# Attention scores in four 64-column matmuls a group instead of eight of 32 columns

## The chip, the core and the metric

The kernel runs on one core of one Trainium2 chip. The metric is the device time of one execution in microseconds; the kernel before takes 1029.15 us (the median of 3 runs, 1028.61 to 1029.83). The core has TensorE (PE in the profile; its weight loads are shown apart, as PEld), VectorE (DVE), ScalarE (ACT), GpSimd (POOL) and SyncE (SP, which here issues DMAs).

## What is computed

For 2048 tokens x of width 512, a gate g mixes an attention block with 32 query heads, one shared key head and one shared value head of 16 columns each, and a feed-forward block:

```
g = sigmoid(sum(x * gate_w))                       # one number per token
q = x @ wq  (32 heads x 16)   k = x @ wk (16)   v = x @ wv (16)
p = softmax(q k^T / 4)                              # per head 2048 x 2048
a = (p v, heads side by side) @ wo
b = silu(x @ w1) @ w2                               # 512 -> 1792 -> 512
out = g * a + (1 - g) * b
```

All of it is float32, and the kernel keeps nearly that accuracy by splitting operands into two 16-bit parts.

## The kernel before, in words

The attention is done in 16 rounds: 4 chunks of 512 tokens times 4 blocks of 8 heads. One round goes through the 2048 keys in 32 steps of 64 keys, and each step does four of the eight heads at a time, twice: `p` counts these half steps, 2 x 32 x 16 = 1024 in all. For each p:

- `scores(p)` (line 1186) writes a PSUM tile `S` of 128 x 1024 float32: the scores of 64 keys for four heads and 512 tokens. The keys `KT` are the weights (the stationary operand), the queries `qb` stream through. One head needs a contraction over 50 rows (16 numbers of q in split parts, and shift rows), so two heads stand in the array one above the other, at rows 0 to 63 and 64 to 127 (index `f`). In the kernel before, a matmul has 50 rows and 32 columns of weights and occupies a tile of 64 rows by 32 columns of the array; eight of them (four column places `m`, two row places `f`) fill the array. Places m = 0 and 1 hold the two halves of the 64 keys for one pair of heads, m = 2 and 3 the same keys for the other pair: they differ only in which part of `qb` they stream. There are two `S` tiles, so scores(p) waits until the exponential of p - 2 has read its own.
- `exponential(p)` (line 1192, on ACT) writes exp of it to a buffer `P` of SBUF.
- `low` (line 1198, on DVE) makes the low part of some of these for a product in two 16-bit parts, and `pv` (line 1223) multiplies by the values, either in float32 or in such parts: weights `VF` or `VP`, 64 rows by 32 columns, again eight tiles filling the array. For a whole step that is 8 matmuls (or 16, in two row halves).

The feed-forward products, the query projections and the output projections run in between. They too are cut into 64 x 32 tiles: `product` (line 832) issues, for four column places, a matmul of a new output on the upper 64 rows and one of an older output on the lower 64 rows. So in the main part of the kernel all matmuls of TensorE, of whatever kind, use tiles of 64 rows by 32 columns, and one pass of eight matmuls streams 512 columns through the full array. `product` and `pv` aren't touched by the change.

Only near the start are there other tile shapes between groups of scores: `begin()` makes the values (128 x 32 tiles, line 1247), transposes them (128 x 64, line 1258) and places the keys (64 x 128, lines 352 and 353), and `early_products()` makes three projections with the whole array (128 x 128, line 836).

What runs when is set at build time. A planner in `attention()` keeps a clock for PE, ACT and DVE, adds assumed durations for each piece (`PASS_S` for a group of scores, `PASS` for a pass, `EXP` for an exponential), and writes the instructions of each engine in the resulting order; on the chip, semaphores alone hold the engines together. The planner's constants are the same in both kernels, and so is the order of everything other than the matmuls and weight loads of the scores.

The last 12 groups of scores (the branch `s >= ends_at`, line 1179) are laid out by token halves and are left as they were. So 1012 of the 1024 groups are concerned. A second pass for inputs out of range stands behind a branch and is not run on these inputs.

Of the kernel before, what the change touches and what calls it, by code (L numbers as in the profile page):

```python
# [53 lines left out]
def kernel(  # L54
# [21 lines left out]
    nc = tc.nc  # L76
# [15 lines left out]
    KT = consts.tile([128, S], F16)  # L92
# [30 lines left out]
    sc = consts.tile([128, 96], F32)  # L123
# [667 lines left out]
    def attention(ctx, scale_of, t_scale, shifts, split_pieces, chores, q_todo, early, gates_):  # L791
# [363 lines left out]
        pvs, state, Os, qtile = {}, {}, {}, {}  # L1155
# [12 lines left out]
        def scores(p):  # L1168
            s, j = divmod(p, 2)
            i, kt = steps[s]  # L1170
            sc = banks[p] = pS.tile([128, 2, 512], F32, name="S")
            if s >= ends_at:
                u, q = (s - ends_at) % PAIRS, (s - ends_at) // PAIRS
                for a in range(2):
                    for m in range(4):
                        for f in range(2):
                            b = 64 * f
                            k0 = (NK - 2 * PAIRS + 2 * u + a) * 64 + 32 * (m % 2)
                            nc.tensor.matmul(sc[32 * m:32 * m + 32, f, 256 * a:256 * a + 256], KT[b:b + 50, k0:k0 + 32],  # L1179
                                             qtile[i][b:b + 50, m // 2, j, 256 * q:256 * q + 256], start=True, stop=True)  # L1180
                return
            for m in range(4):
                for f in range(2):
                    b = 64 * f
                    k0 = kt * 64 + 32 * (m % 2)
                    nc.tensor.matmul(sc[32 * m:32 * m + 32, f], KT[b:b + 50, k0:k0 + 32], qtile[i][b:b + 50, m // 2, j], start=True, stop=True)  # L1186

        def exponential(p):
            s, j = divmod(p, 2)
# [365 lines left out]
        def on_pe(t, x):  # L1555
            _, _, kind, s = x
            length = PASS
            if kind == "S":
                p = n_mm[0]
                i, k = steps[p // 2]  # L1560
                if k >= NKT and i + 1 < len(rounds) and i + 1 not in qtile and (not early or rounds[i + 1][::-1] in shifted):
                    prefetch(i + 1)
                if p % 2 == 0 and k == 0 and q_todo:
                    queue.append(q_todo.pop(0))
                scores(p)
                mm_done[p] = t + PASS_S + LATE
                n_mm[0] += 1
            elif kind == "R":
                length = next(begin_)
                n_begin[0] -= 1  # L1570
            elif kind == "E":
                next(whole_)
                n_early[0] -= 1
            elif kind == "F":
                work.go(t)
            else:
                length = do_pv(*s, t)
            work.others += kind in "SP"
            return length
# [120 lines left out]
```

## Time and profile before

| What | Value |
|---|---|
| median of 3 runs | 1029.15 us |
| profiled execution, first to last instruction | 1033.2 us |
| PE busy | 1012.3 us (98%) |
| ACT busy | 993.1 us (96%) |
| DVE busy | 916.4 us (89%) |
| POOL busy | 62.7 us (6%) |
| matmuls in the profile | 32605, of which 8096 are those of the changed line |
| granted clock of TensorE, mean | 0.998 of full speed |

The profiled execution took 4 us more than the median. In rows of groups, "64*32 64x512" means weights of 64 rows and 32 columns, and 512 streamed columns; busy time is the union of the instructions' spans, so for matmuls that run beside each other it is less than count times mean. The end of a matmul is modelled, while its start is recorded; where spacing matters, starts are read. "issue" as the end of an idle time means that the profile shows nothing that was waited for.

### The profile page before, as it was taken

The numbers are of one execution on the slowest core, as the hardware profiler recorded it, in microseconds if no ns is written. First come the engines' busy times: TensorE is split into PE (matmuls) and PEld (weight loads), VectorE is DVE, ScalarE is ACT, GpSimd is POOL, SyncE is SP. The second block draws the span as 40 slices with busy tenths as digits, with TensorE's granted clock in tenths as the row PEclk, the third lists the DMA queues.
The fourth block names the chain that finished last, engine by engine and source line by source line (L and its number), as shares of the span: only waits on it lengthen the run. The fifth ranks groups of instructions, "written<-read, shape, count | busy, mean of one in ns | idle before, by whom it ended". The sixth has DMA issues, their size and how long they took to land.

```text
span 1033.2 us, 69440 instructions
## 1 busy us (share of the span) xinstructions
PE 1012.3 (98%) x32605; PEld 615.0 (60%) x32605; DVE 916.4 (89%) x1191; ACT 993.1 (96%) x1109; POOL 62.7 (6%) x141
## 2 busy tenths in 40 slices
PE   8999999999999999999999999999999999999996
PEld 7345655565656666656566665566665565565563
DVE  7778887889899999999989899798999889989994
ACT  5899999999999999999999999999999999999994
POOL 5001111100000000000000000000000000000000
PEclk9999999999999999999999999999999999999999
DMA  5122322221011111100101110110111110100001
GB/s 207 53 76 65 93 58 61 70 62 19 15 19 41 39 36 30 20 20 15 35 16 35 50 30 20 30 25 10 34 32 25 33 48 10 35 10 14 10 4 47
DMA packets 28114, 40.12 MB, mean 39 GB/s; under 512 B 5689, under 2 KB 19370, under 8 KB 27818
## 3 DMA queue, kind: packets, MB, share of 16 engines
q0 software_dynamic: 10656, 15.73, 7.3%
q1 hardware_dynamic: 16442, 19.27, 5.9%
q8 instruction: 257, 4.21, 1.7%
q10 hardware_dynamic: 720, 0.59, 0.2%
q14 instruction: 39, 0.32, 0.1%
HBM read 19.98 MB, written 8.25 MB: 27 GB/s over the span
## 4 chain that ended last, share of the span: by engine, by line
PE 71%; issue 19%; ACT 6%; DVE 1%; DMA 1%; POOL 1%; SPq 0%; ACTq 0%; POOLq 0%; DVEq 0%
PE pm L832 26%; PE pv L1223 24%; PE S L1186 17%; ACT P L1192 4%; ACT xs L1192 1%; PE pm L836 1%; DMA xn<-in_A_x_dram 1%; PE pt L336 1%; POOL H L898 1%; PE pv L1211 1%; DMA H<-e 0%; ACT e L886 0%; DVE L L1198 0%; PE S L1179 0%; DVE e L889 0%
## 5 line engine op out<-in xcount | busy, mean ns | idle before, releaser
L1192 ACT ACTIVATE P<-S 128x1024 f32<-128x1024 f32 x764 | 731.4, 1081 | 11.8 <-PE S L1186 7.8
L1186 PE MATMUL S<-qb,KT 50*32 50x512 f16 x8096 | 471.6, 379 | 3.3 <-ACT P L1192 1.7
L1186 PEld LDWEIGHTS <-KT 50*32 50x32 f16 x8096 | 203.3, 90 | 186.6 <-issue 96.7
L1198 DVE TENSOR_TENSOR L<-P 128x1024 f16<-128x1024 f32 x242 | 288.8, 1216 | 20.0 <-ACT P L1192 16.7
L832 PE MATMUL pm<-xs,w1s 64*32 64x512 f16 x5376 | 274.9, 375 | 2.4 <-DVE e L889 1.7
L832 PE MATMUL pm<-w2s,H 64*32 64x512 f16 x5376 | 267.9, 375 | 2.0 <-DVE e L889 1.2
L1192 ACT ACTIVATE xs<-S 128x1024 f32<-128x1024 f32 x260 | 256.8, 1082 | 2.5 <-PE pv L1223 1.1
L1223 PE MATMUL pv<-P,VF 64*32 64x256 f32 (+1 forms) x4880 | 250.6, 450 | 0.3 <-issue 0.3
L832 PEld LDWEIGHTS <-w1s 64*32 64x32 f16 x5376 | 124.7, 92 | 49.8 <-issue 10.8
L832 PEld LDWEIGHTS <-H 64*32 64x32 f16 x5376 | 120.1, 93 | 44.3 <-issue 5.7
L1198 DVE TENSOR_TENSOR raw<-P 128x1024 f16<-128x1024 f32 x104 | 124.8, 1217 | 7.4 <-ACT P L1192 7.1
L1223 PEld LDWEIGHTS pv<-P,VF 64*32 64x32 f32 x4880 | 103.2, 106 | 32.6 <-issue 3.2
L1223 PEld LDWEIGHTS <-VP 64*32 64x32 f16 x3856 | 75.8, 92 | 34.3 <-issue 5.3
L1198 DVE TENSOR_TENSOR L<-xs 128x1024 f16<-128x1024 f32 x72 | 86.5, 1217 | 4.8 <-ACT xs L1192 4.5
L1223 PE MATMUL pv<-L,VP 64*32 64x512 f16 x1256 | 90.6, 375 | 0.0
L832 PE MATMUL pm<-xs,wqs 64*32 64x512 f16 x1152 | 87.0, 375 | 0.0
L1223 PE MATMUL pv<-P,VP 64*32 64x512 bf16 x1384 | 82.7, 387 | 0.0
L1198 DVE TENSOR_TENSOR raw<-xs 128x1024 f16<-128x1024 f32 x64 | 76.9, 1216 | 5.8 <-ACT xs L1192 5.5
L1223 PE MATMUL pv<-xs,VF 64*32 64x256 f32 (+1 forms) x1584 | 76.5, 416 | 0.1
L898 POOL DMA_DIRECT2D H<-e x56 | 30.1, 537 | 733.7 <-DVE e L889 723.2
L832 PE MATMUL pm<-wo_s,O 64*32 64x512 f16 x1440 | 70.4, 375 | 0.1
L1223 PE MATMUL pv<-raw,VP 64*32 64x512 f16 x672 | 54.8, 375 | 0.0
(216 smaller groups left out, 724.1 us busy)
## 6 DMA issues: line engine op xcount, KB each, us to landing
H<-e POOLq DMA_DIRECT2D x56, 128.0 KB, 2.5
raw<-in_B_w_dram POOLq DMA_DIRECT2D x24, 256.0 KB, 3.0
qb<-qd SPq DMA_DIRECT2D x180, 32.0 KB
xn<-in_A_x_dram SPq DMA_DIRECT2D x8, 512.0 KB
out_dram<-acc SPq DMA_DIRECT2D x14, 256.0 KB
qd<-qx SPq DMA_DIRECT2D x13, 256.0 KB
raw<-in_A_wo_dram POOLq DMA_DIRECT2D x4, 256.0 KB, 2.9
qb<-sh SPq DMA_DIRECT2D x60, 2.0 KB
```

Source lines behind the costliest of these rows:

```text
L336: nc.tensor.transpose(pt[:, kt], xn[c].rearrange("p t (d k) -> p t k d", k=KD)[:, t, kt], ident)
L832: nc.tensor.matmul(self.bank[32 * m:32 * m + 32], l(i, rows, 32 * m), r(j, rows), start=first, stop=last)
L836: nc.tensor.matmul(self.bank, l(i, slice(0, 128), 0, 128), r(j, slice(0, 128)), start=first, stop=last)
L898: nc.gpsimd.dma_start(H[:, 0], e)
L1186: nc.tensor.matmul(sc[32 * m:32 * m + 32, f], KT[b:b + 50, k0:k0 + 32], qtile[i][b:b + 50, m // 2, j], start=True, stop=True)
L1192: nc.scalar.activation(probs[s][:, 2 * j:2 * j + 2], banks.pop(p), AF.Exp, scale=scale_of(*rounds[steps[s][0]]))
L1198: nc.vector.tensor_tensor(lows[s, j], probs[s][:, js], upper(probs[s])[:, js], op=OP.subtract)
L1211: nc.tensor.matmul(pvs[i][h][32 * j:32 * j + 32, 256 * q:256 * q + 256], VF[r, NK - 2 * PAIRS + 2 * u + a], probs[s][r, j, 256 * a:256 * a ...
L1223: nc.tensor.matmul(pvs[i][h][32 * j:32 * j + 32, q], a[r], b[r, q], start=k == 0 and n != "B", stop=k == NK - 1 and n in "BMW")
```

## The change

Each of the 1012 groups is now four matmuls with 64 columns of weights each: place m = 0 holds all 64 keys of the step for the first pair of heads, m = 1 for the second pair. A matmul occupies a tile of 64 rows by 64 columns, and four of them fill the array. The scores come out in the same places of `S`, and what is streamed (512 columns for each matmul) is unchanged. A group has four matmuls and four weight loads in place of eight and eight; over the kernel 4048 matmuls and 4048 weight loads fall away.

```
-            for m in range(4):
+            for m in range(2):
                 for f in range(2):
                     b = 64 * f
-                    k0 = kt * 64 + 32 * (m % 2)
-                    nc.tensor.matmul(sc[32 * m:32 * m + 32, f], KT[b:b + 50, k0:k0 + 32], qtile[i][b:b + 50, m // 2, j], start=True, stop=True)
+                    nc.tensor.matmul(sc[64 * m:64 * m + 64, f], KT[b:b + 50, kt * 64:kt * 64 + 64], qtile[i][b:b + 50, m, j], start=True, stop=True)
```

No instruction changes its place: with the matmuls and weight loads of the scores left out, the order of every engine's instructions is the same before and after. In that order 998 groups of scores stand alone between other work of TensorE, and only seven times do two follow one another: 1005 stretches of scores. On 18 of them the work ahead, and on 20 the work behind, has one of the other shapes of the start; at all other borders it is a matmul of 64 x 32.

## The prediction

> **What bounds the kernel now.** I read the page's busy shares first, then the groups of instructions kept apart by form, then the timeline of PE and of its weight loads. The page:
>
> ```profile
> PE 1012.3 (98%) x32605; PEld 615.0 (60%) x32605; DVE 916.4 (89%) x1191; ACT 993.1 (96%) x1109; POOL 62.7 (6%) x141
> L1192 ACT ACTIVATE P<-S 128x1024 f32<-128x1024 f32 x764 | 731.4, 1081 | 11.8 <-PE S L1186 7.8
> ```
>
> Two engines look full. From the first group of scores to near the end (27.47 to 1012 us), in the view of busy time by stretch (us, then PE, PEld, DVE, ACT, POOL with their instructions, granted clock, DMA share, GB/s):
>
> ```profile
> 27.47:1012.00 984.53, 976.48 (x32008) 589.51 (x32007) 886.43 (x1111) 971.01 (x1076) 49.08 (x90) 1.00 0.14 34
> ```
>
> ACT is idle for only 984.5 - 971.0 = 13.5 us of it: ACT, with its 1024 exponentials, is what sets the pace. PE's busy time overstates its work, since the recorded span of a matmul overlaps the next. What PE needs is passes times spacing. The spacing, from starts in PE's timeline (start, us, what, count):
>
> ```profile
> 404.99 0.58 PE L1186 MATMUL S<-qb,KT 50*32 50x512 f16 x8
> 405.21 1.01 PE L832 MATMUL pm<-w2s,H 64*32 64x512 f16 x24
> 405.86 0.57 PE L1186 MATMUL S<-qb,KT 50*32 50x512 f16 x8
> 406.08 1.22 PE L832 MATMUL pm<-w2s,H 64*32 64x512 f16 x32
> 406.94 0.57 PE L1186 MATMUL S<-qb,KT 50*32 50x512 f16 x8
> ```
>
> Eight matmuls of 64 x 32 are one pass: a group of scores takes 405.21 - 404.99 = 0.22 us, three feed-forward passes 0.65 and four 0.86, so 0.216 each. A float32 pass over 512 columns takes twice that (from the next fence but one: 16 matmuls from 37.76 to 38.62, 0.43 each). The number of passes, by form (count | busy us, mean ns | idle before):
>
> ```profile
> L1186 PE MATMUL S<-qb,KT 50*32 50x512 f16 x8096 | 471.6, 379 | 3.3 <-ACT P L1192 1.7 <-ACT xs L1192 0.8 <-issue 0.3
> L832 PE MATMUL pm<-xs,w1s 64*32 64x512 f16 x5376 | 274.9, 375 | 2.4 <-DVE e L889 1.7 <-issue 0.4 <-DVE acc L813 0.2
> L832 PE MATMUL pm<-w2s,H 64*32 64x512 f16 x5376 | 267.9, 375 | 2.0 <-DVE e L889 1.2 <-issue 0.7
> L1223 PE MATMUL pv<-P,VF 64*32 64x256 f32 x3168 | 133.9, 375 | 0.3 <-issue 0.3
> L1223 PE MATMUL pv<-P,VF 64*32 64x512 f32 x1712 | 117.9, 589 | 0.0
> L1223 PE MATMUL pv<-L,VP 64*32 64x512 f16 x1256 | 90.6, 375 | 0.0
> L832 PE MATMUL pm<-xs,wqs 64*32 64x512 f16 x1152 | 87.0, 375 | 0.0
> L1223 PE MATMUL pv<-P,VP 64*32 64x512 bf16 x1384 | 82.7, 387 | 0.0
> L832 PE MATMUL pm<-wo_s,O 64*32 64x512 f16 x1440 | 70.4, 375 | 0.1
> L1223 PE MATMUL pv<-xs,VF 64*32 64x256 f32 x1280 | 55.8, 375 | 0.1
> L1223 PE MATMUL pv<-raw,VP 64*32 64x512 f16 x672 | 54.8, 375 | 0.0
> L1223 PE MATMUL pv<-xs,VP 64*32 64x512 bf16 x544 | 32.3, 387 | 0.0
> L1223 PE MATMUL pv<-xs,VF 64*32 64x512 f32 x304 | 20.9, 589 | 0.0
> ```
>
> Counts over 8: 1012 groups of scores x 0.22 = 222.6 us; line 832, 13344 matmuls, 1668 passes x 0.216 = 360.3; values over 256 float32 columns, 4448, 556 x 0.216 = 120.1; in 16-bit parts, 3856, 482 x 0.216 = 104.1; over 512 float32 columns, 2016, 252 x 0.43 = 108.4. Together 915.5 us; the small forms in the stretch (36 whole-array matmuls, values, keys, the tail's quarter groups) add under 20 by their counts. So of 984.5 us PE needs some 925 and has about **60 us of slack**, in small pieces: anything that costs PE less than 60 us in all can vanish behind ACT, and anything above shows.
>
> **The change, part by part.** Removed: 4048 matmuls and 4048 weight loads. The streamed columns stay 512 for each matmul, and four tiles of 64 x 64 fill the array as eight of 64 x 32 did, so a group remains one pass of 0.22 us; no columns of weights are saved either (4 x 64 = 8 x 32). ACT's and DVE's instructions are the same. So the part removed is worth at most ACT's 13.5 us of idle time; I take nothing, as ACT's waits for scores are 7.8 us in the row above.
>
> Added: the array's tile shape is now another in every group of scores than in the work around it. Before, all of the main part is 64 x 32, and the weights of the next pass are loaded while the current one streams. The trace has other shapes only near the start, and these are the rows that decide. First a change in the columns alone (64 x 32 to 64 x 128, as rows 64 stay), then to the whole array and back, then to 128 x 32 and back:
>
> ```profile
> 36.66 0.40 PE L1186 MATMUL S<-qb,KT 50*32 50x512 f16 x8
> 36.99 0.39 PE L352 MATMUL pm<-wo_s 64*128 64x512 f16 x1
> 37.22 0.38 PE L353 MATMUL pm<-wo_s 64*128 64x512 f16 x1
> 37.53 0.41 PE L1186 MATMUL S<-qb,KT 50*32 50x512 f16 x8
> 37.76 1.04 PE L1223 MATMUL pv<-P,VF 64*32 64x512 f32 x16
> 38.62 0.40 PE L1186 MATMUL S<-qb,KT 50*32 50x512 f16 x8
> ...
> 42.23 0.61 PE L836 MATMUL pm<-xs,wqs 128*128 128x512 f16 x2
> 42.76 0.41 PE L1186 MATMUL S<-qb,KT 50*32 50x512 f16 x8
> 43.10 0.82 PE L836 MATMUL pm<-xs,wqs 128*128 128x512 f16 x3
> 43.85 0.41 PE L1186 MATMUL S<-qb,KT 50*32 50x512 f16 x8
> 44.20 0.61 PE L836 MATMUL pm<-xs,wqs 128*128 128x512 f16 x2
> 44.73 1.09 PE L1223 MATMUL pv<-P,VF 64*32 64x512 f32 x16
> ```
>
> From 36.66 to 37.53 three passes stand: 3 x 0.216 = 0.648, but 0.87 went by: 0.222 us for two changes of shape, 0.111 each (the border S to L352 took 0.33 instead of 0.22, the border L353 to S 0.31). From 42.23 to 44.73 nine passes, 1.944 us of work in 2.50: 0.556 for five changes, 0.111 each. And
>
> ```profile
> 30.11 0.41 PE L1186 MATMUL S<-qb,KT 50*32 50x512 f16 x8
> 30.45 0.83 PE L1247 MATMUL pm<-xs,wo_s 128*32 128x512 f16 x12
> 31.22 0.41 PE L1186 MATMUL S<-qb,KT 50*32 50x512 f16 x8
> ```
>
> four passes in 1.11 us instead of 0.864: 0.246 for two, 0.123 each. None of these borders has a wait that the profile names. The weight loads show why (PEld, same times; second row a border without a change of shape):
>
> ```profile
> 36.99 0.09 PEld L352 LDWEIGHTS <-wo_s 64*128 64x128 f16 x1 [0.64 <-issue]
> 37.55 0.33 PEld L1223 LDWEIGHTS pv<-P,VF 64*32 64x32 f32 x16
> ```
>
> For L352 the load begins at 36.99, with its matmul, and only when the pass before has run out; the value weights begin at 37.55, 0.21 us ahead of their matmuls at 37.76. A change of shape lets no weights in ahead, and the array stands empty for a tenth of a microsecond.
>
> The Trainium skill states this as a rule that speaks against the change: "TensorEngine Tiling (Array Packing)", section Key Properties, says that changing the tiling mode, and not merely the tile, drains TensorE. The trace agrees for the three pairs of shapes above, at 0.11 to 0.12 us; no run here shows 64 x 64 beside 64 x 32 yet.
>
> The number of changes: 1005 stretches of scores have 2010 borders, 38 of which change the shape already; 1972 are new. 64 x 64 against 64 x 32 isn't in the trace. Its price lies between nothing (were it not another shape to the hardware) and the whole overlap of two passes (a matmul's 379 ns less the 216 of spacing, 0.163 us). I take 0.111, from the row that is nearest, 64 rows and other columns: **1972 x 0.111 = 219 us** of new work for PE.
>
> What hides it: PE's 60 us of slack. The gaps that PE makes for ACT (a score tile not yet read) close as ACT ceases to be the bound; gaps from other causes, like feed-forward results (2 us each in the rows of line 832) or the start, stay. I take 50 of 60 as used up. Then PE is the bound, ACT waits for scores, and the planned order, made for a pace that ACT sets, is merely late. DVE and the DMAs have no new work and gain time. Sum against the profiled execution: 1033.2 + 219 - 50 = 1202 us; the median stood 4 us below that execution, so **1198 us**. With 0.09 a change (just under the smaller border above) and all slack used, 1029 + 177 - 60 = 1146; with 0.123 and half of it, 1029 + 243 - 30 = 1242.
>
> **Rivals.**
>
> *No change of shape between 64 x 64 and 64 x 32* (ends on the other side). If the hardware keeps its weights-ahead when only the column count doubles within the same rows, nothing is added and 8096 fewer instructions go through PE; ACT loses some of its 13.5 us of idle time: 1018 to 1029, say 1027 us. It decides wherever a change costs below 60 / 1972 = 0.03 us. For it: the exact pair isn't in the trace. Against: the pair 64 x 32 and 64 x 128, rows alike, pays 0.111.
>
> *Only one direction pays*, as a 64 x 64 load may have to wait for two narrow tiles while a narrow load finds its tile free: 986 x 0.111 = 109, less 50: 1029 + 59 = 1088 us. Against: both borders paid in every row above (0.33 and 0.31 for 0.22).
>
> *The whole overlap is lost*, 0.163 a change, or the four wide loads, now exposed, are slower than the narrow ones: 321 - 50, 1300 us. Against: L352 and L353, with 128 columns of weights, start 0.23 apart and not later. "TensorE: Matmul & The Clock Gate", section Single matmul latency, of the Trainium skill gives a constant of about 166 ns beyond the streaming of a warm matmul; a full drain at each change would by that be an estimated 327 us. The trace's borders, 0.11, are below it.
>
> **How the numbers follow.** The main case has 0.80, no change of shape 0.08, one direction 0.06, the whole overlap 0.06. Predicted 1198 us; the main case's own bounds are 1146 to 1242, and the range, 1150 to 1250, holds most of that and leaves the three rivals out. 0.2% (2 us) is about what a measurement of this kernel can tell from no change. Faster by more comes from half of the second case, 0.04; within 0.2% from its other half, 0.04; slower 0.92.
>
> **What would show it.** PE matmuls fall to 32605 - 4048 = 28557. In the timeline a feed-forward pass to a group of scores takes 0.31, and scores to the next pass 0.33; weight loads of the scores begin with their matmuls, with idle time of PEld before them in nearly every group. ACT's busy time stays near 993 us but its share falls to about 83%, and its idle time, now some 200 us, is ended by PE's scores. If instead the borders read 0.22 with loads ahead, the first rival holds; if they read 0.33 but the span rose by far less than 170 us, the slack was mis-sized; borders of 0.38 mean the whole overlap.

## The result, and the profile after

The changed kernel takes 1248.75 us (median of 4 runs, 1248.57 to 1249.66) against 1028.88 us before, measured with it (median of 4 runs): 1.2142 times as long, 95% interval 1.2126 to 1.2159. The prediction was 1198 us with a range of 1150 to 1250, so the direction and the cause were right and the loss came out 220 us instead of 169. That the time still lies inside the range, 1 us below its upper end, is luck: it is above the 1242 us that the forecast gave as the upper bound of its main case.

From the page of the changed kernel (lines as before, less one from line 1186 on):

```profile
PE 1231.5 (99%) x28557; PEld 422.0 (34%) x28557; DVE 925.8 (74%) x1191; ACT 1072.0 (86%) x1109; POOL 62.6 (5%) x141
PE 97%; DMA 1%; DVE 1%; ACT 0%; issue 0%
L1191 ACT ACTIVATE P<-S 128x1024 f32<-128x1024 f32 x764 | 773.8, 1025 | 113.2 <-PE S L1185 74.9
L1185 PE MATMUL S<-qb,KT 50*64 50x512 f16 x4048 | 414.9, 400 | 0.3 <-ACT P L1191 0.2
L1185 PEld LDWEIGHTS <-KT 50*64 50x64 f16 x4048 | 114.4, 103 | 471.8 <-issue 471.8
```

The second line is the share of engines in the chain that ended last. TensorE is now the bound: 97% of that chain, where the kernel before had

```profile
PE 71%; issue 19%; ACT 6%; DVE 1%; DMA 1%; POOL 1%; SPq 0%; ACTq 0%; POOLq 0%; DVEq 0%
```

ACT's wait for scores went from 7.8 to 74.9 us in the first of its two rows, while TensorE's scores hardly wait for ACT any more (0.3 us of idle time in all). The last row holds the cause: the loader of weights is idle for 471.8 us just before the scores' weights, 0.47 us for each of 1012 groups, and the profile names nothing that it waits for. In the timeline of PE, with full passes (columns: start, us, what, count):

```profile
481.87 0.41 PE L1185 MATMUL S<-qb,KT 50*64 50x512 f16 x4
482.20 0.66 PE L1222 MATMUL pv<-P,VF 64*32 64x256 f32 x16
482.66 0.42 PE L1222 MATMUL pv<-raw,VP 64*32 64x512 f16 x8
483.01 0.41 PE L1185 MATMUL S<-qb,KT 50*64 50x512 f16 x4
483.36 0.66 PE L1222 MATMUL pv<-P,VF 64*32 64x256 f32 x16
483.81 0.42 PE L832 MATMUL pm<-w2s,H 64*32 64x512 f16 x8
484.16 0.41 PE L1185 MATMUL S<-qb,KT 50*64 50x512 f16 x4
484.50 0.84 PE L832 MATMUL pm<-w2s,H 64*32 64x512 f16 x24
485.27 0.41 PE L1185 MATMUL S<-qb,KT 50*64 50x512 f16 x4
485.62 0.84 PE L832 MATMUL pm<-w2s,H 64*32 64x512 f16 x24
486.39 0.41 PE L1185 MATMUL S<-qb,KT 50*64 50x512 f16 x4
486.73 1.06 PE L832 MATMUL pm<-w2s,H 64*32 64x512 f16 x32
487.71 0.41 PE L1185 MATMUL S<-qb,KT 50*64 50x512 f16 x4
```

Scores to the next pass take 0.34 us (484.16 to 484.50) where 0.22 stood; three feed-forward passes and the border to the scores 0.77 (484.50 to 485.27) where 0.65 stood. From 484.16 to 487.71 are 13 passes, 2.81 us at 0.216, in 3.55 us: 0.74 us for six changes of shape, 0.124 each. From 481.87 to 484.16, among value products, eight passes, 1.73 us, took 2.29: 0.14 for each of four changes. The weight loads beside it (PEld):

```profile
484.16 0.11 PEld L1185 LDWEIGHTS <-KT 50*64 50x64 f16 x4 [0.42 <-issue]
484.50 0.35 PEld L832 LDWEIGHTS <-H 64*32 64x32 f16 x24 [0.23 <-issue]
```

At both borders the loads start with their matmuls, after an idle time. Within the stretch of 24 they run ahead again.

### The profile page after: what moved, and what is told of

Its sections match the earlier page's. It is cut to its first block, busy times and chain, and to the rows that moved or that the text cites. A ratio compares the mean times of both kernels' runs of the same rounds, so it can differ in the third digit from the quotient of the medians.

```text
span 1246.6 us, 61343 instructions
## 1 busy us (share of the span) xinstructions
PE 1231.5 (99%) x28557; PEld 422.0 (34%) x28557; DVE 925.8 (74%) x1191; ACT 1072.0 (86%) x1109; POOL 62.6 (5%) x141
## 4 chain that ended last, share of the span: by engine, by line
PE 97%; DMA 1%; DVE 1%; ACT 0%; issue 0%
PE pm L832 35%; PE pv L1222 31%; PE S L1185 27%; DMA xn<-in_A_x_dram 1%; PE pm L836 1%; PE pv L1210 0%; PE pm L427 0%; PE pt L336 0%; PE pm L1246 0%; PE S L1179 0%; PE pk L502 0%; PE pm L1257 0%; ACT P L1191 0%; DVE e L889 0%; PE pv L1649 0%
## 5 line engine op out<-in xcount | busy, mean ns | idle before, releaser
L1191 ACT ACTIVATE P<-S 128x1024 f32<-128x1024 f32 x764 | 773.8, 1025 | 113.2 <-PE S L1185 74.9
L1185 PE MATMUL S<-qb,KT 50*64 50x512 f16 x4048 | 414.9, 400 | 0.3 <-ACT P L1191 0.2
L1185 PEld LDWEIGHTS <-KT 50*64 50x64 f16 x4048 | 114.4, 103 | 471.8 <-issue 471.8
L832 PE MATMUL pm<-xs,w1s 64*32 64x512 f16 x5376 | 260.8, 380 | 0.8 <-DVE e L889 0.7
L832 PEld LDWEIGHTS <-w1s 64*32 64x32 f16 x5376 | 76.1, 90 | 76.8 <-issue 57.1
L832 PEld LDWEIGHTS <-H 64*32 64x32 f16 x5376 | 74.9, 90 | 75.4 <-issue 56.5
L1197 DVE TENSOR_TENSOR raw<-xs 128x1024 f16<-128x1024 f32 x64 | 77.3, 1220 | 15.8 <-ACT xs L1191 12.2
L1222 PEld LDWEIGHTS pv<-P,VF 64*32 64x32 f32 x4880 | 68.2, 105 | 54.5 <-issue 39.2
L889 DVE SCALAR_TENSOR_TENSOR e<-e,pm 128x512 f32<-128x512 f32 x56 | 38.5, 687 | 53.4 <-ACT e L886 53.2
L813 DVE SCALAR_TENSOR_TENSOR acc<-pm,g,acc 128x512 f32<-128x512 f32 x48 | 36.0, 750 | 55.3 <-PE pm L832 55.2
L1222 PEld LDWEIGHTS <-VP 64*32 64x32 f16 x3856 | 51.7, 90 | 55.1 <-issue 36.6
```

The source lines that it names most:

```text
L813: nc.vector.scalar_tensor_tensor(a, po, gate[:, m:m + 1], a, op0=OP.mult, op1=OP.add)
L832: nc.tensor.matmul(self.bank[32 * m:32 * m + 32], l(i, rows, 32 * m), r(j, rows), start=first, stop=last)
L889: nc.vector.scalar_tensor_tensor(e, e, 1.0, o.bank, op0=OP.add, op1=OP.mult)
L1185: nc.tensor.matmul(sc[64 * m:64 * m + 64, f], KT[b:b + 50, kt * 64:kt * 64 + 64], qtile[i][b:b + 50, m, j], start=True, stop=True)
L1191: nc.scalar.activation(probs[s][:, 2 * j:2 * j + 2], banks.pop(p), AF.Exp, scale=scale_of(*rounds[steps[s][0]]))
L1197: nc.vector.tensor_tensor(lows[s, j], probs[s][:, js], upper(probs[s])[:, js], op=OP.subtract)
```

## Experiments

Theory A, that of the forecast: each change of tile shape holds up the whole array for about 0.12 us, a wide pass in itself costs no more than a narrow one, and only what exceeds TensorE's slack shows. Theory B, the rival: the wide matmuls are slow in themselves. The experiments ran on three chips, on which the kernel before took 1040.27, 1040.86 and 1042.86 us; each is compared with its runs there. Expectations that count from 1029 us are to be read 11 to 14 us higher on these chips.

### Wide feed-forward passes, with and without wide scores

```
-                nc.tensor.matmul(self.bank[32 * m:32 * m + 32], l(i, rows, 32 * m), r(j, rows), ...)
+                nc.tensor.matmul(self.bank[64 * m:64 * m + 64], l(i, rows, 64 * m, 64), r(j, rows), ...)
...
-                for m in range(4):      # in go()
+                for m in range(2):
```

in the changed kernel:

> Scores as changed, and the feed-forward and projection passes (line 832) also in 64 x 64 tiles; the value products stay 64 x 32. By the order of instructions there are now 1234 more changes of tile shape than in the kernel before (the changed kernel has 1972 more), although 1668 more passes are wide. Theory A (a change of shape costs, the wide pass itself doesn't): the changed kernel pays (1246.6 - 1033.2 + some 30 of slack) / 1972 = 0.124 us a change, so 1029 + 1234 x 0.124 - 28 = about 1154 us. Theory B (the wide matmuls themselves are slow, 0.249 us more a pass whatever stands beside them): (1012 + 1668) x 0.249 = 667, less the slack: about 1668 us.

and in the kernel before:

> Scores as in the kernel before (eight of 64 x 32), and the passes of line 832 in 64 x 64 tiles instead: 1466 more changes of shape than before. Theory A: 1029 + 1466 x 0.124 - 28 = about 1183 us, slower than with scores and these passes both wide, though fewer passes are wide. Theory B: 1668 x 0.249 - 28 = 387, about 1416 us, and faster than with both wide. Of the border itself: if what is lost is the run-out of the old pass, a scores pass of eight narrow matmuls, whose last starts some 22 ns after its first, gives 0.33 to the next pass as before, and a wide pass of four, 10 ns, gives less skew and the 0.34 that the changed kernel shows on leaving a wide pass.

Measured: 1162.75 us with both wide (1.118 times the 1040.27 us of before, 1.113 to 1.123), 1185.70 with only the feed-forward passes wide (1.140, 1.135 to 1.145). Both lie within 9 us of theory A, counted from 1029 us or from 1040, and hundreds from B; widening the scores *as well* makes the second kernel 23 us faster, as the borders between scores and feed-forward passes vanish and 232 fewer changes are left in all. The timeline with both wide shows a border of either kind:

```profile
480.45 0.41 PE L1185 MATMUL S<-qb,KT 50*64 50x512 f16 x4
480.79 0.42 PE L1222 MATMUL pv<-P,VP 64*32 64x512 bf16 x8
481.04 1.04 PE L1222 MATMUL pv<-P,VF 64*32 64x512 f32 x16
482.01 0.41 PE L1185 MATMUL S<-qb,KT 50*64 50x512 f16 x4
482.25 0.82 PE L832 MATMUL pm<-xs,w1s 64*64 64x512 f16 x12
482.90 0.39 PE L1185 MATMUL S<-qb,KT 50*64 50x512 f16 x4
483.12 0.82 PE L832 MATMUL pm<-xs,w1s 64*64 64x512 f16 x12
```

The same wide scores go to narrow value products in 0.34 us and to wide feed-forward passes in 0.22 (482.90 to 483.12), or 0.24 where the scores' own weights had not been loaded ahead (482.01 to 482.25). With only the feed-forward passes wide, narrow scores give 0.33 to a wide pass, as expected, and 0.34 where the scores themselves stand right behind a change.

### The wide pass by itself

```
+            for _ in range(2):      # the changed kernel's loop over m and f, twice
             for m in range(2):
```

> The changed kernel with each group of wide scores issued twice in a row (the second writes the same numbers again): 1012 more wide passes, no more changes of shape. Theory A: a wide pass after a wide pass costs 0.216, so 1248.75 + 1012 x 0.216 = about 1467 us. Theory B: 0.216 + 0.249 for each, about 1719 us.

Measured 1465.18 us, 2 us from theory A: (1465.18 - 1248.75) / 1012 = 0.214 us for an added wide pass. In its timeline

```profile
481.13 0.63 PE L1186 MATMUL S<-qb,KT 50*64 50x512 f16 x8
481.69 0.63 PE L832 MATMUL pm<-w2s,H 64*32 64x512 f16 x16
```

two wide passes and the border take 0.56, one and the border 0.34. Theory B falls.

### Does a change of shape hold up the whole array?

```
-                for m in range(4):
-                    if self.new and self.i < len(self.new.mm):
-                        self.new.product(self.i, lo, m, self.i == 0, False)
+                if self.new and self.i < len(self.new.mm):
+                    for m in range(2):
+                        self.new.product(self.i, lo, m, self.i == 0, False, 64)    # 64 columns, rows 0 to 63
+                for m in range(4):
                     ...  # the older output, 32 columns, rows 64 to 127, as before
```

> Passes of line 832 with the newer output's matmuls (rows 0 to 63) in two tiles of 64 x 64, issued first, and the older output's (rows 64 to 127) in four of 64 x 32; scores as before. If the whole array has one shape at a time, every such pass has two changes of shape inside, and its halves no longer stream beside each other: two stretches of 0.31 to 0.34 us where 0.216 stood, 1668 x 0.43 = 717 us more, about 1700 us or above. If a change of shape only holds up the tiles that overlap the old ones, the lower rows are never concerned and it comes out near the kernel with all of line 832 wide, 1186 us, or faster.

Measured 1975.07 us, 1.89 times the kernel before (1.876 to 1.902). The weight loads in its timeline (PEld), each beginning with its matmuls:

```profile
480.40 0.11 PEld L832 LDWEIGHTS <-H 64*64 64x64 f16 x2 [0.42 <-issue]
480.73 0.10 PEld L832 LDWEIGHTS <-H 64*32 64x32 f16 x4 [0.23 <-issue]
481.06 0.11 PEld L832 LDWEIGHTS <-H 64*64 64x64 f16 x2 [0.23 <-issue]
481.39 0.10 PEld L832 LDWEIGHTS <-H 64*32 64x32 f16 x4 [0.23 <-issue]
481.72 0.11 PEld L832 LDWEIGHTS <-H 64*64 64x64 f16 x2 [0.23 <-issue]
482.05 0.10 PEld L832 LDWEIGHTS <-H 64*32 64x32 f16 x4 [0.23 <-issue]
482.06 0.11 PEld L1187 LDWEIGHTS <-KT 50*32 50x32 f16 x8
```

A pass takes 0.66 us instead of 0.216 (480.40 to 481.06 to 481.72): 0.33 for its two wide matmuls in rows 0 to 63 and 0.33 for its four narrow ones in rows 64 to 127, the time of a border each. They don't run beside each other, though they share no row. In the last two lines the shape is the same on both sides, and there the scores start 0.01 us behind the narrow matmuls and run beside them. So one shape holds for the whole array. (The clock granted to TensorE was 1.00 from 470 to 490 us, but 0.83 to 0.87 on average in the four runs, for a reason that the runs don't show. Time multiplied by granted clock, an estimate of the time at full clock, is 1684 to 1696 us, near the 1700 of the expectation.)

### How much is hidden

In the kernel before, only every second, fourth or eighth group of scores is wide:

```
+            if p % 2 == 0:          # or p % 4, p % 8
+                ...                 # the four wide matmuls, and return
             for m in range(4):
```

> Only every second group of scores is wide (506 of 1012): 991 more changes of shape than before. Theory A with some 30 us hidden: 1029 + 991 x 0.124 - 28 = about 1124 us. If nothing is hidden and each change costs 220 / 1972 = 0.112: 1029 + 111 = 1140 us.

> Every fourth group is wide (253): 498 more changes. Theory A: 62 us more work for TensorE, some 28 of it hidden: about 1063 us. If nothing is hidden and a change costs 0.112: 1085 us.

> Every eighth group is wide (127): 249 more changes. Theory A: 31 us more work for TensorE, about as much as its slack, so most is hidden: 1030 to 1042 us. If nothing is hidden and a change costs 0.112: 1057 us.

And the kernel before with other work added to TensorE, no change of shape:

```
+            for _ in range(2):      # the kernel before's loop over m and f, twice
             for m in range(4):
```

> The kernel before with each group of narrow scores issued twice in a row: 1012 more narrow passes of 0.219 us, 221.6 us of TensorE work, no change of shape. It asks how much added work of TensorE is hidden behind ScalarE. If some 28 us are (as 1972 changes of 0.124 would need): about 1222 us. If the 50 us of the forecast are: 1201 us. If nothing is hidden, and a change of shape costs only 0.111 as the forecast had it: 1251 us.

All against the kernel before on the same chip; the work is the new changes of shape times 0.124 us, or the added passes times 0.219:

| Kernel | Added work of TensorE, us | Time, us | Over the kernel before, us | Hidden, us |
|---|---|---|---|---|
| every 8th group wide | 249 x 0.124 = 30.9 | 1049.43 | 8.6 | 22 |
| every 4th | 498 x 0.124 = 61.8 | 1071.26 | 30.4 | 31 |
| every 2nd | 991 x 0.124 = 122.9 | 1127.02 | 86.2 | 37 |
| both wide | 1234 x 0.124 = 153.0 | 1162.75 | 122.5 | 31 |
| feed-forward wide | 1466 x 0.124 = 181.8 | 1185.70 | 145.4 | 36 |
| all scores wide, repeated here | 1972 x 0.124 = 244.5 | 1249.59 | 206.7 | 38 |
| narrow groups twice | 1012 x 0.219 = 221.6 | 1261.65 | 221.4 | 0 |

The intervals of the first three ratios are 1.0057 to 1.0107, 1.0268 to 1.0339 and 1.0795 to 1.0868. From every second group to all, 981 more changes cost 120.5 us: 0.123 each, the timeline's price found again from times alone, as the hidden part hardly differs between the two. The hidden part is 22 us at first and levels off at 31 to 38 us. The eighth came out above the expected 1030 to 1042 us; counted from the 1041 us of its chip that is 1042 to 1054, which holds 1049. Still, 22 of 30.9 us is not nearly all. It may be that slack lies in small pieces, and that a change of shape doesn't always fall where one is; this wasn't tested. The other case, nothing hidden and 0.112 a change, would add 28, 56 and 111 us in the first three rows, where 8.6, 30.4 and 86.2 were measured.

The last row falls out of line. Taken alone it fits the case that nothing is hidden (1251 us, or 1262 counted from 1040), which the first three rows exclude. ACT was 85% busy and so not what held TensorE. The timeline, PE and then PEld, shows another loss:

```profile
836.05 0.85 PE L832 MATMUL pm<-w2s,H 64*32 64x512 f16 x24
836.70 0.41 PE L1187 MATMUL S<-qb,KT 50*32 50x512 f16 x8
837.75 0.41 PE L1187 MATMUL S<-qb,KT 50*32 50x512 f16 x8 [0.63 <-issue]
```

```profile
836.49 0.31 PEld L1187 LDWEIGHTS <-KT 50*32 50x32 f16 x9
837.75 0.11 PEld L1187 LDWEIGHTS <-KT 50*32 50x32 f16 x7 [0.95 <-issue]
```

Between the two identical halves of one group, with nothing to wait for, neither a matmul nor a load starts for a microsecond. I numbered the starts of all of TensorE's instructions in order, the 97 that are neither matmuls nor weight loads included, and looked at those from 66 us on, to 30 us before the end: 69 of the 86 holes of over 0.4 us stand at one and the same place of a period of 256 instructions (after number 193, counted modulo 256), 41.1 us together from start to start. The page's row of instruction fetches has the same period:

```profile
q8 instruction: 320, 5.24, 1.7%
```

5.24 MB in 320 packets is 16.4 KB a packet, and over the 81402 matmuls and loads some 64 bytes an instruction: 256 instructions a packet. That made theory I: a narrow pass, 16 instructions in 0.216 us, uses instructions about as fast as they come. The packets' own times bear it out: each of the 69 holes ends 1.2 to 1.6 us after a packet of this queue has landed, and so do the holes at that place in two executions of the kernel before. Where there is no hole, TensorE passes the place hardly sooner either (1.1 us after the packet at the least), while in the changed kernel and with the wide scores twice it passes 2.6 us or more after it.

### Testing the instruction supply

```
+            for half in range(2):
+                for m in range(4 - 2 * half):     # the second time only the column places 0 and 1
```

> The kernel before with each group of scores issued and then its first four matmuls (two column places, both row places) once more: the same 1012 added passes of 0.219 us as with the whole group issued twice, for two column places at least, but 4048 matmuls and 4048 weight loads fewer. If TensorE's time alone counted, as with the whole group twice: 1262 us. By theory I, the 30 us that the twice-issued kernel loses at every 256th instruction mostly go: about 1232 us.

Measured 1223.18 us, 38 us less than with the whole group twice; 41 of the 221.6 us of work are hidden, as with the wide kernels, and one hole of over 0.4 us is left at that place of the period. 8 us more went than the 30 of the expectation. The shorter holes may be those: at that place the trace with the whole group twice has 60 gaps of 0.1 to 0.4 us, 13.5 us together, and this one 13, of 2.0 us. But these passes also leave two column places free, and in the timeline matmuls of the next pass start there among those of the repeat; what part of the 38 us comes from that was not separated.

> The kernel before once more, for a profile on the chip of the other experiments, where it took 1040 us and not 1029. If TensorE there runs short of instructions now and then (theory I: a pass of eight narrow matmuls and eight weight loads uses instructions about as fast as they can be fetched), the extra 11 us show as TensorE stalls that end without a wait, at 256 instructions' distance from each other or a multiple of it; if ScalarE or DMAs are slower there, as longer exponentials or waits for them.

> The changed kernel on this chip. It has an eighth fewer instructions on TensorE and longer passes, so by theory I it isn't short of them and takes 1249 us here too, 209 us over the kernel before instead of 220. If this chip is slower in everything, it takes 1262.

Both ran on the third chip. The kernel before took 1045.94 us in this one execution (span 1043.9) and shows 27 holes at that place of the period, 15.8 us together; the profile shown ahead of the prediction (span 1033.2) has 12, 6.5 us. That is 9.3 of the 10.7 us between the two spans. One of them, within a group of scores:

```profile
223.97 0.38 PE L1186 MATMUL S<-qb,KT 50*32 50x512 f16 x1
225.01 0.41 PE L1186 MATMUL S<-qb,KT 50*32 50x512 f16 x7 [0.66 <-issue]
```

The changed kernel took 1249.59 us here and 1248.75 there, with a ratio of 1.1994 (1.1949 to 1.2039) in place of 1.2142, and has one hole at that place. So the kernel before is the one that varies, and the changed kernel isn't short of instructions. That the holes are late fetches rests on their period, on the landing of the packets before their ends, and on what makes them go; the profile itself names no cause for a hole.

## Why the prediction was right, and where it was off

**What bounds the kernel.** That PE has slack held: adding 31 us of work to PE cost 8.6. That ACT alone sets the pace is less sure, as the chain before has PE at 71% and ACT at 6%. The size of the slack was wrong. "PE needs some 925 and has about 60 us of slack": in the runs of the forecast 244.5 us of work cost 219.9, so only 25 us were hidden, and 38 in the later ones. The traces show it directly. The stretches from one group of scores to the next have the same content in both kernels. Grouped by that content (925 of 1011 stretches, whose content stands at least three times), those of the kernel before lose 35 us beyond the 15th percentile of their group, and those of the changed kernel 6. So the step that was mis-sized is the sum of passes, read as if all the rest were slack. Two of its terms are known: the small forms were put at 10 of "under 20" us and take 19 by their starts, and every pass was put at 0.216, although starts after the 241 bf16 passes are some 0.23 apart, 3 us in all. The rest of the difference is not taken apart. And a part of the gaps (6.5 us in holes at the 256-instruction period) was never a wait for ACT. It went all the same, as the changed kernel uses its instructions more slowly; there the gain was counted under a wrong name.

**Removed: nothing gained.** The added wide pass at 0.214 us confirms that four wide matmuls take no less and no more than a pass of eight narrow ones. One thing was overlooked: 8096 fewer instructions are worth something in a kernel that runs short of them. Against 244.5 us of borders it doesn't show by itself.

**The price of a change, 0.111.** The mechanism, a change of shape lets no weights in ahead, held: the loads of 1004 of the 1012 groups of scores begin within 0.02 us of their matmuls. And 64 x 64 beside 64 x 32 is a change like the three seen before. The term was mis-sized: 0.124, which makes 244.5 instead of 219 us. (Over the 925 stretches the two changes of a stretch cost 0.246 us at the 15th percentile, 0.123 each; the dearer borders after float32 value products are among them.) The reason is in the rows that it was taken from. The starts of a pass's matmuls are some 3 ns apart, and what a border fixes is the time from the *last* start of the old pass to the first of the new: in the changed kernel 306 ns after narrow feed-forward passes (10th to 90th percentile of 494 borders 305 to 306), with eight matmuls whose last starts 23 ns after the first. The 64 x 128 pass, from whose rows I took the price, is one matmul, and has 306 with nothing to add; a whole-array pass has 309. The same 306 holds in the kernel with wide feed-forward passes, four matmuls and 10 ns. To this comes the first pass after a change, whose loads are exposed: 10 ns for narrow 16-bit weights, 21 to 24 for float32, 24 for the 64-column weights of the scores. With the wide scores issued twice the 24 ns are gone from the border behind them, which has 306. The rows of the forecast had neither these 24 ns nor the 10 ns between the starts of a wide pass.

**What hides it, 50 of 60 us.** 25 in those runs. With the price these make the miss: 25.5 us of price and 25 us of slack are the 50 us between 1198 and 1248.75. Both lie just outside the bounds that the forecast gave them, 0.123 and 30 us. My step down by 4 us from the profiled execution to the median plays no part in this account, which goes by medians throughout.

**The rivals.** No change of shape: excluded, each border costs 0.12. Only one direction: both pay (0.33 into the scores, 0.34 out of them). The whole overlap, 0.163: above what was seen, though borders beside float32 value products come near, 0.14. The Trainium skill, "TensorEngine Tiling (Array Packing)", Key Properties, has the rule that changing the mode drains TensorE. The traces agree, with 306 ns from the last start of one shape to the first of the next, and the runs add that this holds with no row in common. The Trainium skill's "TensorE: Matmul & The Clock Gate", Single matmul latency, has the constant behind the estimate of 327 us. That was too high, as 244.5 us were lost.

**What would show it.** Matmuls 28557 as forecast; borders 0.33 and 0.34 for 0.31 and 0.33; the loads beside their matmuls. ACT's busy time didn't stay at 993 us: it is 1072, at 86% and not 83%. The exponentials now stand apart: their recorded spans overlap by 15 us in all where they overlapped by 147. With that the mean of one fell from 1081 to 1025 ns in the first row, but the union of their spans grew.

## What to carry to other kernels

Keep TensorE in one tile shape through a loop: fewer, wider matmuls saved nothing here, where a pass still streams the same columns, and each change of shape cost about 0.12 us of the whole array. Take the price of a border from passes built like those that will stand there, and count slack by what an added load of known size really hides, not by a sum of nominal spacings; look in that load's trace for losses of its own. If a loop of small tiles shows holes with no wait, number its instructions before looking for a slow engine.

## What the runs showed of the hardware that I had not expected

- One tile shape holds for the whole array: tiles of 64 x 64 in rows 0 to 63 and of 64 x 32 in rows 64 to 127 take turns, 0.66 us for a pass of 0.216.
- A border runs from the last start of the old shape: 306 ns at full clock to the first start of the new one after narrow passes of 16-bit numbers.
- TensorE with eight narrow matmuls and eight weight loads in 0.216 us is at the edge of its supply of instructions: holes of 0.4 to 1 us at a period of 256 instructions, 6.5 us in one execution of the kernel before, 15.8 in another, 41.1 with the narrow groups issued twice, and 0.6 with half of that repeat left out. They end 1.2 to 1.6 us after a packet of instructions has landed.
